# A Strassen step for the second product of a feed-forward block, with attention by thirds of the queries, on one Trainium2 core

## The chip, the core and the metric

The kernel runs on one core of a Trainium2 chip. A core has TensorE (matrix products into PSUM), VectorE, ScalarE and GpSimd (work on columns of 128 partitions), and DMA queues that move data between the device's memory and the on-chip memory. Each engine takes its own instructions in order; they wait for each other through semaphores. The metric is the device time of one execution in microseconds (us), and lower is better.

In the profiles "PE" is TensorE, "PEld" its loading of weights (the stationary operand), "DVE" VectorE, "ACT" ScalarE, "POOL" GpSimd and "SP" the queue that issues the DMAs. "L448" is line 448 of the kernel.

## The reference

Attention with a mask by clusters, then two products with an ELU between. Batch 4, 8 heads, 768 positions, head size 64, 16 clusters, model size 512, inner size 2048, so 3072 tokens in the second part.

```python
def _attn_ref(q, k, v, centroids):
    # q_n, k_n, c_n: rows of q, k, centroids divided by their norms
    q_assign = np.argmax(np.einsum('bhsd,hcd->bhsc', q_n, c_n), axis=-1)
    k_assign = np.argmax(np.einsum('bhsd,hcd->bhsc', k_n, c_n), axis=-1)
    mask = q_assign[:, :, :, None] == k_assign[:, :, None, :]
    scores = scale * np.matmul(q, k.transpose(0, 1, 3, 2))
    scores = np.where(mask, scores, -1000000000.0)
    # softmax over the last axis
    return np.matmul(attn, v)

def _moe_ref(x, w_in, w_out):           # x: (3072, 512)
    h = x @ w_in                        # first product, 512 -> 2048
    g = np.where(h > 0.0, h, np.exp(np.minimum(h, 0.0)) - 1.0)
    return (g @ w_out).astype(np.float32)   # second product, 2048 -> 512
```

The two weight matrices arrive as 64-bit floats, everything else as 32-bit floats. The products run in fp32, but for the mask, which is a product of one-hot rows in bf16.

## The kernel before

The core of it, cut. `b` is the batch, `half` a half of the queries (`HS` = 384), `pr` a pair of heads; `FC` = 16 and `KC` = 4 are the inner and model sizes in blocks of 128, `NT` = 6 the blocks of keys.

The 64-bit weights come in 32 pieces of 128 x 512. Each piece is turned into fp32 by four VectorE, two ScalarE and one GpSimd instruction, with one piece begun while the one before is ended. `ex` has two buffers.

```python
def weight_steps():
    for n in range(len(pieces) + 1) if wide else ():
        if n > 0:
            to = pieces[n - 1][0]
            ex = exps[n - 1]
            nc.scalar.activation(to, to.bitcast(U32), Act.Identity, scale=2.0**-20, bias=one)
            nc.scalar.activation(ex, ex, Act.Relu, scale=8.0, bias=off)
        if n < len(pieces):
            high = words[n][0][:, :, 1]
            e = exps[n] = loads.tile([P, WC], U32, name="ex", tag="ex", bufs=2)
            nc.vector.tensor_scalar(pieces[n][0].bitcast(U32), high, 0xFFFFF, None, op0=Alu.bitwise_and)
            nc.vector.tensor_scalar(e, high, 0x7FF00000, None, op0=Alu.bitwise_and)
        if n > 0:
            w, place, limit = words.pop(n - 1)
            nc.vector.scalar_tensor_tensor(ex, w[:, :, 1], 0x80000000, ex, ...)
            nc.vector.scalar_tensor_tensor(to, w[:, :, 0], 2.0**-52, to, ...)
            nc.gpsimd.tensor_tensor(to, to, ex.bitcast(F32), op=Alu.mult)
            places.append((place, limit))   # the place may take the next piece
            ask()
        yield
```

Attention for block n (batch, half, pair): scores with keys on the partitions, exponentials, the product with v, the row sums (by a product with ones; from pass 6 on VectorE adds the six tiles first), the reciprocal, the scaled result `xT`.

```python
def scores(n):
    for kt in range(NT):
        s = banks()                       # 2 PSUM banks of 512 columns; 3 such pairs
        for e in range(2):                # two heads, on 64 rows of the array each
            nc.tensor.matmul(s[:, e, :HS], lhsT=T[i, 1][rows, ts(kt, P)], rhs=T[i, 0][rows, cols], ...)
        for e in range(2):                # the mask, bf16
            nc.tensor.matmul(s[:, e, :HS], lhsT=hot[b, 1][rows, side(pr, e), ts(kt, P)], rhs=qm[n][rows], ...)
        p = pu[n, kt] = probs.tile([P, 2, HS], F32, name="p", tag="p")
        nc.scalar.activation(p, s[:, :, :HS], Act.Exp, scale=SCALE)

def values(n):
    # ... 12 matmuls of 384 columns into o_bank, 2 (or 12) into d for the row sums
    nc.scalar.copy(x, o_bank[:, :HS])
    nc.scalar.activation(r, d[:, :HS], Act.Copy, accum_out=d_sum[:, n : n + 1])
    nc.vector.reciprocal(r, r)
    nc.gpsimd.tensor_tensor(x, x, r, op=Alu.mult)
```

The feed-forward part of one half of a batch, in four groups of steps:

```python
def hidden(n):                            # 8 of these: 256 inner columns each
    h = banks()
    for ch in range(KC):
        for e in range(2):
            nc.tensor.matmul(h[:, e, :HS], lhsT=w_in[:, ch, ts(2 * n + e, P)], rhs=xT[b * NPR + ch, half], ...)
    t = g[n] = gtp.tile([P, 2, HS], F32, name="gT", tag="gT")
    nc.scalar.activation(t, h[:, :, :HS], Act.Exp)
    nc.gpsimd.tensor_scalar(t, t, 1.0, 0.0, op0=Alu.min, op1=Alu.max)
    finish()                              # the VectorE step of the block before
    lag.append(lambda: nc.vector.scalar_tensor_tensor(t, t, -1.0, h[:, :, :HS], op0=Alu.add, op1=Alu.max))

def outer(t, part):                       # 128 tokens, 4 of 16 inner blocks
    o = f_bank if t == 1 else o_bank
    for f in range(4 * part, 4 * part + 4):
        nc.tensor.matmul(o, lhsT=g[f // 2][:, f % 2, ts(t, P)], rhs=w_out[:, f], ...)   # 512 columns
    if part == 3:
        nc.scalar.copy(o_sb, o)
        nc.sync.dma_start(out[...], o_sb)
```

The loop of passes. A pass runs the values of the block before, the scores of its own block, and the group of feed-forward steps that lies four passes back.

```python
for n in range(len(blocks) + LAG):        # 32 blocks, LAG = 4
    if n <= len(blocks) and n > 0:
        values(n - 1)
    # ... loads of q, k, v ahead
    if n < len(blocks):
        scores(n)
    # ... check(n - 1): a ScalarE sum over r, for a test at the end
    # ... masks(n + 1), sums(n) from n = 6 on, the turning of the next batch's q and k
    main = groups[n - LAG] if n >= LAG else []
    if n < LAG:
        weigh(4)                          # four conversion steps
    for m, step in enumerate(main):
        step()
        # ... a part of the next batch's routing
        if m < 4:
            weigh(2)
```

Of the kernel before, what the change touches and what calls it, by code (L numbers as in the profile page):

```python
# [9 lines left out]
F32 = mybir.dt.float32  # L10
# [8 lines left out]
P = 128  # L19
# [11 lines left out]
def kernel(  # L31
# [24 lines left out]
    with tc.If(good < P):  # L56
        general_path(tc, c, q, k, v, out)
# [3 lines left out]
def main_path(ctx, tc, c, q, k, v, centroids, moe_w_in, moe_w_out, out):  # L61
# [6 lines left out]
    HS = S // 2  # L68
    NPR = H // 2
# [3 lines left out]
    assert D == 64 and NC == 16 and H * NC == P and S % (2 * P) == 0 and DM == H * D and NPR == 4  # L73
# [5 lines left out]
    probs = ctx.enter_context(tc.tile_pool(name="probs", bufs=6))  # L79
    work = ctx.enter_context(tc.tile_pool(name="work", bufs=2))  # L80
    xtp = ctx.enter_context(tc.tile_pool(name="xtp", bufs=6))
    gtp = ctx.enter_context(tc.tile_pool(name="gtp", bufs=FC // 2))
# [11 lines left out]


    pairs = [(b, pr) for b in range(B) for pr in range(NPR)]
    raw = {}
    spare = c["w_out"].rearrange("p f m -> p (f m)")
    used = 0

    def take(n):
        nonlocal used
        used += n
        return spare[:, used - n : used]

    def load(name, i, staged=False):
        b, pr = pairs[i]
        src = {"q": q, "k": k, "v": v}[name]
        if staged:
            t = take(2 * NT * D)  # L110
        else:
            t = loads.tile([P, 2 * NT * D], F32, name=f"{name}_raw", tag=name, bufs=2)
# [27 lines left out]
    for name in "qk":  # L140
        for i in range(NPR):
            load(name, i, staged=i >= 2)
# [49 lines left out]
    r_sum = const.tile([P, 2 * len(pairs)], F32, name="r_sum")  # L192
    d_sum = const.tile([P, 2 * len(pairs)], F32, name="d_sum")
# [70 lines left out]
    for n in range(2):  # L264
        places.append((loads.tile([P, 2 * WC], F32, name="words", tag=f"words{n}"), len(pieces)))
    while used + 2 * WC <= FC * DM:
        limit = into + used // DM - 1
        places.append((take(2 * WC), limit))
# [3 lines left out]
    def weigh(n):  # L272
        for _ in range(n):
            next(rest, None)

# [68 lines left out]
    def masks(n):  # L344
        b, half, pr = blocks[n]
        qm[n] = route.tile([P, HS], BF16, name="qm", tag="qm", bufs=2)
        for e in range(2):
# [4 lines left out]
                hot[b, 0][rows, side(pr, e), half * HS : (half + 1) * HS],  # L352
# [7 lines left out]
    blocks = [(b, half, pr) for b in range(B) for half in range(2) for pr in range(NPR)]  # L360
    pu, osum, xT, rs = {}, {}, {}, {}

    def scores(n):
        b, half, pr = blocks[n]
        i = b * NPR + pr
        cols = slice(half * HS, (half + 1) * HS)
        for kt in range(NT):
            s = banks()
            for e in range(2):
                rows = slice(64 * e, 64 * e + 64)  # L370
                nc.tensor.matmul(  # L371
                    s[:, e, :HS],
                    lhsT=T[i, 1][rows, ts(kt, P)],
                    rhs=T[i, 0][rows, cols],
                    start=True,
                    stop=False,
                )
            for e in range(2):
                rows = slice(64 * e, 64 * e + 64)
                nc.tensor.matmul(  # L380
                    s[:, e, :HS],
                    lhsT=hot[b, 1][rows, side(pr, e), ts(kt, P)],
                    rhs=qm[n][rows],
                    start=False,
                    stop=True,
                )
            p = pu[n, kt] = probs.tile([P, 2, HS], F32, name="p", tag="p")
            nc.scalar.activation(p, s[:, :, :HS], Act.Exp, scale=SCALE)  # L388

    def sums(n):  # L390
        to = osum[n] = work.tile([P, 2, HS], F32, name="psum", tag="psum", bufs=1)
        nc.vector.tensor_tensor(to, pu[n, 0], pu[n, 1], op=Alu.add)
        for kt in range(2, NT):
            nc.vector.tensor_tensor(to, to, pu[n, kt], op=Alu.add)  # L394

    def values(n):

        b, half, pr = blocks[n]
        i = b * NPR + pr
# [3 lines left out]
        def row_sums(p, kt, last):  # L403
            for e in range(2):
                nc.tensor.matmul(  # L405
                    d[64 * e : 64 * e + 64, :HS],
                    lhsT=ones,
                    rhs=p[:, e],
# [4 lines left out]
        for kt in range(NT):  # L413
            for e in range(2):
                nc.tensor.matmul(  # L415
                    o_bank[64 * e : 64 * e + 64, :HS],
                    lhsT=raw["v", n][:, e, kt],
                    rhs=pu[n, kt][:, e],
# [3 lines left out]
            if summed is None:  # L422
                row_sums(pu[n, kt], kt, NT - 1)
        if summed is not None:
            row_sums(summed, 0, 0)
        x = xT[i, half] = xtp.tile([P, HS], F32, name="xT", tag="xT")
        nc.scalar.copy(x, o_bank[:, :HS])  # L427
        r = work.tile([P, HS], F32, name="r", tag="r", bufs=1)
        nc.scalar.activation(r, d[:, :HS], Act.Copy, accum_out=d_sum[:, n : n + 1])  # L429
# [4 lines left out]
    def check(n):  # L434

        seen_r = work.tile([P, HS], BF16, name="seen_r", tag="seen_r", bufs=1)
# [3 lines left out]
    def mlp(b, half):  # L440

        g, lag = {}, []

        def hidden(n):
            h = banks()
            for ch in range(KC):
                for e in range(2):
                    nc.tensor.matmul(  # L448
                        h[:, e, :HS],
                        lhsT=w_in[:, ch, ts(2 * n + e, P)],  # L450
# [15 lines left out]
        def finish():  # L466
            for step in lag:
                step()
# [342 lines left out]
```

## Time and profile before

The time is 1067.61 us (median of three; 1067.3 at the lowest). One of the three took 3830.59 us. The profiled execution has a span of 1067.0 us.

| What | Value | How to read it |
|---|---|---|
| TensorE busy | 1033.4 us, 4211 matmul instructions | busy time is the union of the instructions, which overlap |
| First product, 128x384 | 334.5 us, 1024 instructions | an fp32 matmul is two instructions |
| Second product, 128x512 | 224.6 + 112.8 us, 768 instructions | in two groups, by PSUM bank |
| Scores, fp32 and bf16 | 167.1 + 65.9 us, 768 + 384 instructions | two at a time, on halves of the array's rows |
| Product with v | 136.0 us, 768 instructions | two at a time, on halves of the columns |
| VectorE, ScalarE, GpSimd busy | 418.6, 365.0, 143.5 us | they work in order, so a wait of one step holds all behind it |

The groups of instructions give the mean time of one instruction from its start to its end. For TensorE this is longer than the time from one to the next. The chain of waits follows the run back from its last instruction, at each step to what released it. A table of stretches gives, for a stretch of time, the busy time and the number of instructions of each engine, the granted TensorE clock, the share of DMA and the rate in GB/s.

### The profile page before, as it was taken

Reading aid. Unit: us, or ns where it says so; the run is one execution under the profiler, and the core shown is the slowest. Engines: PE = TensorE matmul, PEld = TensorE weight load, DVE = VectorE, ACT = ScalarE, POOL = GpSimd, SP = SyncE. Lnnn points to the kernel's source line nnn. Section 1 sums busy time; section 2 is a strip of 40 time slices with the busy share of each in tenths; the row PEclk is TensorE's granted clock in tenths of the full one; section 3 lists DMA queues with packets and bytes.
Section 4 is the critical chain, followed back from the end, with each engine's and each line's share of the span. In section 5 each row is a group of like instructions: output and inputs, shape, how many; then the busy total and the mean of one; then the engine's idle time right before and its main releaser. Section 6 shows DMA issues by size and latency. Waiting matters only on the chain.

```text
span 1067.0 us, 10433 instructions
## 1 busy us (share of the span) xinstructions
PE 1033.4 (97%) x4211; PEld 512.3 (48%) x4211; DVE 418.6 (39%) x516; ACT 365.0 (34%) x579; POOL 143.5 (13%) x136
## 2 busy tenths in 40 slices
PE   6979897999999999999999999999999999999997
PEld 4434453445544455445544455444554455444543
DVE  4665856353332343273432134355331233321110
ACT  4876464213332333114333223323331234321100
POOL 0233432001100011001110011000110011100100
PEclk9999898999999999999999999999999999999999
DMA  9374424000202112000202021001000000000000
GB/s 287 97 195 143 117 76 76 25 35 1 45 25 44 47 33 45 25 10 25 45 15 55 35 45 30 25 15 36 15 15 25 20 15 15 16 10 20 1 10 22
DMA packets 99590, 49.01 MB, mean 46 GB/s; under 512 B 83152, under 2 KB 92368, under 8 KB 99536
## 3 DMA queue, kind: packets, MB, share of 16 engines
q1 hardware_dynamic: 99536, 48.28, 17.5%
q8 instruction: 35, 0.57, 0.2%
q14 instruction: 19, 0.16, 0.0%
HBM read 41.98 MB, written 6.29 MB: 45 GB/s over the span
## 4 chain that ended last, share of the span: by engine, by line
PE 89%; DVE 4%; POOL 2%; ACT 2%; issue 1%; DMA 1%; POOLq 0%; ACTq 0%
PE banks L448 29%; PE o_bank L474 21%; PE banks L371 12%; PE f_bank L474 10%; PE o_bank L415 10%; PE banks L380 3%; PE banks L405 2%; PE banks L307 1%; POOL w_out L259 1%; DVE ex L253 1%; POOL w_in L259 1%; DVE ex L250 1%; PE banks L296 1%; ACT p L388 1%; DVE w_out L256 1%
## 5 line engine op out<-in xcount | busy, mean ns | idle before, releaser
L448 PE MATMUL banks<-xT,w_in 128*128 128x384 f32 x1024 | 334.5, 488 | 0.4 <-POOL xT L431 0.4
L448 PEld LDWEIGHTS banks<-xT,w_in 128*128 128x128 f32 x1024 | 193.4, 190 | 139.5 <-issue 7.3
L474 PE MATMUL o_bank<-w_out,gT 128*128 128x512 f32 x512 | 224.6, 596 | 0.0
L430 DVE RECIPROCAL r<-r 128x384 f32<-128x384 f32 x32 | 81.6, 2551 | 295.3 <-ACT r L429 295.3
L371 PE MATMUL banks<-qT,kT 64*128 64x384 f32 x768 | 167.1, 514 | 18.4 <-DVE gT L461 9.9
L388 ACT ACTIVATE p<-banks 128x768 f32<-128x768 f32 x192 | 154.2, 811 | 28.1 <-PE banks L380 28.0
L474 PEld LDWEIGHTS o_bank<-w_out,gT 128*128 128x128 f32 x512 | 96.0, 190 | 122.6 <-issue 122.3
L461 DVE SCALAR_TENSOR_TENSOR gT<-gT,banks 128x768 f32<-128x768 f32 x64 | 61.0, 954 | 215.3 <-POOL gT L458 215.3
L415 PE MATMUL o_bank<-p,v_raw 128*64 128x384 f32 x768 | 136.0, 491 | 0.0
L457 ACT ACTIVATE gT<-banks 128x768 f32<-128x768 f32 x64 | 51.8, 810 | 231.4 <-PE banks L448 231.4
L394 DVE TENSOR_TENSOR psum<-psum,p 128x768 f32<-128x768 f32 x104 | 115.3, 1109 | 11.3 <-DVE psum L394 0.5
L431 POOL TENSOR_TENSOR xT<-xT,r 128x384 f32<-128x384 f32 x32 | 46.5, 1452 | 494.6 <-DVE r L430 494.6
L474 PE MATMUL f_bank<-w_out,gT 128*128 128x512 f32 x256 | 112.8, 593 | 0.0
L371 PEld LDWEIGHTS banks<-qT,kT 64*128 64x128 f32 x768 | 69.9, 196 | 77.1 <-issue 41.2
L458 POOL TENSOR_SCALAR gT<-gT 128x768 f32<-128x768 f32 x64 | 53.9, 843 | 278.7 <-ACT gT L457 278.7
L415 PEld LDWEIGHTS o_bank<-p,v_raw 128*64 128x64 f32 x768 | 52.3, 137 | 77.3 <-issue 76.8
L474 PEld LDWEIGHTS f_bank<-w_out,gT 128*128 128x128 f32 x256 | 48.4, 190 | 61.6 <-issue 61.6
L483 ACT COPY o_sb<-o_bank 128x512 f32<-128x512 f32 x16 | 9.4, 585 | 200.1 <-PE o_bank L474 200.1
L380 PE MATMUL banks<-qm,hot 64*128 64x384 bf16 x384 | 65.9, 332 | 1.0 <-DVE hot L336 1.0
L427 ACT COPY xT<-o_bank 128x384 f32<-128x384 f32 x32 | 15.2, 474 | 130.6 <-PE o_bank L415 130.6
L350 ACT ACTIVATE qm<-hot,minus,big 64x384 bf16<-64x384 bf16 x64 | 44.7, 698 | 4.1 <-DVE hot L336 3.3
L380 PEld LDWEIGHTS <-hot 64*128 64x128 bf16 x384 | 20.3, 97 | 28.7 <-issue 3.3
(88 smaller groups left out, 432.6 us busy)
## 6 DMA issues: line engine op xcount, KB each, us to landing
v_raw<-in_v_dram SPq DMA_DIRECT2D x32, 384.0 KB, 3.2
out_dram<-o_sb SPq DMA_DIRECT2D x24, 256.0 KB, 2.0
w_out<-in_moe_w_in_dram SPq DMA_DIRECT2D x10, 512.0 KB, 5.8
q_raw<-in_q_dram SPq DMA_DIRECT2D x48, 96.0 KB, 3.8
k_raw<-in_k_dram SPq DMA_DIRECT2D x48, 96.0 KB, 3.3
w_out<-in_moe_w_out_dram SPq DMA_DIRECT2D x9, 512.0 KB, 3.5
words<-in_moe_w_out_dram SPq DMA_DIRECT2D x7, 512.0 KB, 3.5
words<-in_moe_w_in_dram SPq DMA_DIRECT2D x6, 512.0 KB, 4.1
```

What stands on the lines that cost most here:

```text
L371: nc.tensor.matmul(s[:, e, :HS], lhsT=T[i, 1][rows, ts(kt, P)], rhs=T[i, 0][rows, cols], start=True, stop=False,)
L380: nc.tensor.matmul(s[:, e, :HS], lhsT=hot[b, 1][rows, side(pr, e), ts(kt, P)], rhs=qm[n][rows], start=False, stop=True,)
L388: nc.scalar.activation(p, s[:, :, :HS], Act.Exp, scale=SCALE)
L394: nc.vector.tensor_tensor(to, to, pu[n, kt], op=Alu.add)
L415: nc.tensor.matmul(o_bank[64 * e : 64 * e + 64, :HS], lhsT=raw["v", n][:, e, kt], rhs=pu[n, kt][:, e], start=(kt == 0), stop=(kt == NT - 1),)
L430: nc.vector.reciprocal(r, r)
L431: nc.gpsimd.tensor_tensor(x, x, r, op=Alu.mult)
L448: nc.tensor.matmul(h[:, e, :HS], lhsT=w_in[:, ch, ts(2 * n + e, P)], rhs=xT[b * NPR + ch, half], start=(ch == 0), stop=(ch == KC - 1),)
L457: nc.scalar.activation(t, h[:, :, :HS], Act.Exp)
L458: nc.gpsimd.tensor_scalar(t, t, 1.0, 0.0, op0=Alu.min, op1=Alu.max)
L461: lambda: nc.vector.scalar_tensor_tensor(t, t, -1.0, h[:, :, :HS], op0=Alu.add, op1=Alu.max)
L474: nc.tensor.matmul(o, lhsT=g[f // 2][:, f % 2, ts(t, P)], rhs=w_out[:, f], start=(f == 0), stop=(f == FC - 1),)
```

## The change

The second product G x W (G: 256 tokens by 2048; W: 2048 by 512) is cut into 2 x 2 blocks and computed with seven block products in place of eight. With G's rows as tokens, G = [[a, b], [c, d]] (blocks of 128 tokens x 1024) and W = [[e, f], [g, h]] (1024 x 256), it needs sums of blocks of W, made once, and sums of blocks of G and of products, made for every 256 tokens. They are put on VectorE, GpSimd and ScalarE. Each block product is 8 matmuls of 256 columns in fp32.

So that 256 tokens come at a time, the queries of a batch are taken in three thirds of 256 in place of two halves of 384. There are 48 blocks of attention in place of 32, each with 256 columns, and scores of two key blocks share a pair of banks, so that an exponential takes 1024 columns. The four hidden blocks of a third have 512 inner columns each. A third's feed-forward part is again four groups: hidden blocks 0 and 1; hidden blocks 2 and 3; block products 1 to 4; block products 5 to 7.

The weights are now all converted before the pass that has the first block products (pass 6): four steps in each of passes 0 to 3, five after each step of passes 4 and 5, and the sums of the weights in pass 6. The 64-bit pieces wait in the space of the weight sums and of the second weight matrix, in 14 places in place of 7. The first batch's q and k wait in the space of g.

The diff, cut to its core:

```diff
+    NQ = 3
+    QS = S // NQ
-    probs = ctx.enter_context(tc.tile_pool(name="probs", bufs=6))
+    probs = ctx.enter_context(tc.tile_pool(name="probs", bufs=NT // 2))
-    gtp = ctx.enter_context(tc.tile_pool(name="gtp", bufs=FC // 2))
+    g = const.tile([P, FC, QS], F32, name="gT")
+    g_sum = const.tile([P, FC // 2, P], F32, name="g_sum")
+    w_sum = const.tile([P, 3, FC // 2, QS], F32, name="w_sum")
 ...
+    def sum_weights(half):
+        of = slice(half * FC // 4, (half + 1) * FC // 4)
+        e_, f_, g_, h_ = (x[:, of] for x in w_parts())
+        t1, t2, t4 = (w_sum[:, n, of] for n in range(3))
+        nc.gpsimd.tensor_tensor(t1, f_, e_, op=Alu.subtract)
+        nc.gpsimd.tensor_tensor(f_, h_, f_, op=Alu.subtract)
+        nc.vector.tensor_tensor(t2, h_, t1, op=Alu.subtract)
+        nc.vector.tensor_tensor(t4, g_, t2, op=Alu.subtract)
 ...
     def scores(n):
-        for kt in range(NT):
+        for u in range(NT // 2):
             s = banks()
+            for m in range(2):
+                kt = 2 * u + m
 ...
+            p = pu[n, u] = probs.tile([P, 2, 2 * QS], F32, name="p", tag="p")
+            nc.scalar.activation(p, s, Act.Exp, scale=SCALE)
 ...
+    def hidden(b, third, n):
+        h = banks()
+        hf = h.rearrange("p a (f s) -> p (a f) s", f=2)
+        for ch in range(KC):
+            for f in range(4):
+                nc.tensor.matmul(hf[:, f], lhsT=w_in[:, ch, ts(4 * n + f, P)], rhs=xT[b, third][:, ch], ...)
+        t = g[:, 4 * n : 4 * n + 4]
+        nc.scalar.activation(t, hf, Act.Exp)
+        nc.gpsimd.tensor_scalar(t, t, 1.0, 0.0, op0=Alu.min, op1=Alu.max)
+        finish()
+        lag.append(lambda: elu(n, t, hf))
+
+    def elu(n, t, hf):
+        nc.vector.scalar_tensor_tensor(t, t, -1.0, hf, op0=Alu.add, op1=Alu.max)
+        if n < 2:      # c becomes a - c
+            nc.vector.tensor_tensor(t[:, :, P:], t[:, :, :P], t[:, :, P:], op=Alu.subtract)
+        else:          # g_sum = d - (a - c)
+            nc.vector.tensor_tensor(g_sum[:, 4 * n - 8 : 4 * n - 4], t[:, :, P:],
+                g[:, 4 * n - 8 : 4 * n - 4, P:], op=Alu.subtract)
+
+    def product(to, left, right, more=False):
+        for f in range(FC // 2):
+            nc.tensor.matmul(to[:, :QS], lhsT=left[:, f], rhs=right[:, f], ...)
+    # outer: seven of these
+    #  1 product(o_bank, a_, e_)              ScalarE copies; VectorE: a_ = g_sum + a_
+    #  2 product(f_bank, c_, f_)              ScalarE copies
+    #  3 product(o_bank, b_, g_, more=True)   ScalarE copies; VectorE: b_ = b_ - g_sum
+    #  4 product(f_bank, d_, t4, more=True)   ScalarE copies
+    #  5 product(f_bank, g_sum, t2)           VectorE adds
+    #  6 product(o_bank, a_, t1)              VectorE and GpSimd add
+    #  7 product(f_bank, b_, h_)              VectorE and GpSimd add, two stores
+
+    def mlp(b, third):
+        steps = [lambda n=n: hidden(b, third, n) for n in range(FC // 4)]
+        yield steps[:2]
+        yield steps[2:] + [finish]
+        yield from outer(b, third)
 ...
         if n < LAG:
             weigh(4)
+        if n == LAG + 2:
+            weigh(100)
+            for half in range(2):
+                sum_weights(half)
 ...
-            if m < 4:
-                weigh(2)
+            if n < LAG + 2:
+                weigh(5)
```

A second path, for inputs that the main path can't take, reloads a part of the second weight matrix, as the sums are made in its place. It isn't taken here.

## The prediction

> **What bounds the kernel now.** I read the granted clock first (one core, 0.990: nothing to correct), then the page's busy times and slices, the chain of waits, and the stretches of time. The page says TensorE is the bound:
>
> ```profile
> PE 1033.4 (97%) x4211; PEld 512.3 (48%) x4211; DVE 418.6 (39%) x516; ACT 365.0 (34%) x579; POOL 143.5 (13%) x136
> PE   6979897999999999999999999999999999999997
> PEclk9999898999999999999999999999999999999999
> PE 89%; DVE 4%; POOL 2%; ACT 2%; issue 1%; DMA 1%; POOLq 0%; ACTq 0%
> ```
>
> The 97% hides two regimes. A table of stretches (length, busy us and count by engine, clock, DMA share, GB/s), cut at the first instruction of the second product (178.45) and at the end of the last big matmul group (1060.20), shows them:
>
> ```profile
> 178.45:1060.20 881.75, 881.39 (x3391) 433.38 (x3390) 305.32 (x322) 258.09 (x414) 87.26 (x83) 1.00 0.10 25
> 0.00:178.45 178.45, 151.93 (x822) 78.92 (x822) 113.09 (x194) 106.35 (x164) 56.23 (x53) 0.94 0.55 148
> ```
>
> After 178.45 TensorE waits for nothing. Before it TensorE is busy for 151.93 of 178.45 us, and part of that at a lower clock (0.94 on the mean). The chain of waits in time order explains it. First a piece of the start, then a piece of the later stretch:
>
> ```profile
> 48.99 1.39 POOL w_in L259
> 52.12 1.39 POOL w_in L259
> 55.24 1.40 POOL w_in L259
> ...
> 144.17 1.39 POOL w_out L259
> ...
> 147.29 1.27 POOL w_out L259
> ...
> 541.59 4.02 PE o_bank L415 x24
> 546.26 0.84 PE banks L371 x4
> 551.30 13.93 PE o_bank L474 x32
> 565.23 6.87 PE f_bank L474 x16
> 572.10 4.02 PE o_bank L415 x24
> ```
>
> In the start the chain runs through the conversion of the 64-bit weights: VectorE, ScalarE, VectorE, GpSimd for each of 32 pieces, one piece per 3.13 us (48.99 to 52.12 to 55.24). Later it is a clock of 572.10 - 541.59 = 30.51 us per pass: attention for one pair of heads and half of the queries, plus a quarter of one half's feed-forward.
>
> **What a matmul of 256 columns costs.** The groups by line and shape give the rates:
>
> ```profile
> L448 PE MATMUL banks<-xT,w_in 128*128 128x384 f32 x1024 | 334.5, 488 | 0.4 <-POOL xT L431 0.4
> L474 PE MATMUL o_bank<-w_out,gT 128*128 128x512 f32 x512 | 224.6, 596 | 0.0
> L448 PEld LDWEIGHTS banks<-xT,w_in 128*128 128x128 f32 x1024 | 193.4, 190 | 139.5 <-issue 7.3
> L371 PEld LDWEIGHTS banks<-qT,kT 64*128 64x128 f32 x768 | 69.9, 196 | 77.1 <-issue 41.2
> ```
>
> Each fp32 matmul is two instructions, and the mean (488, 596) is latency, as they overlap. The throughput comes from the chain: 64 of 384 columns in 20.84 us is 325.6 ns, 48 of 512 columns in 20.80 us (13.93 + 6.87) is 433.3 ns. That is 0.842 ns per column and about 2.5 ns fixed, so 256 columns cost about 217.9 ns. A weight load of 190 ns fits under that, if it starts with the matmul before it.
>
> **What the Trainium skill says.** "TensorE: Matmul & The Clock Gate", section "Back-to-back issue gap", has a fixed part of about 2.5 ns per matmul when warm; the two rates above agree. Its section "Step-by-step: what each phase is for" says that the next weights load while a matmul runs; the trace agrees, since 190 ns loads cost nothing beside 325.6 ns matmuls, though no run so far shows 256 columns. Its section "HAM oscillation — how this bites in real kernels" says that a gap of over about 3.4 us puts the clock back to half; the trace agrees, with a clock of 0.94 in the start and 1.00 after. "SBUF — State Buffer", section "Who interferes with whom", says that a VectorE instruction with two SBUF inputs contends with GpSimd's reads; the trace agrees: GpSimd's multiply of 128x384 takes 1.0 us in the start and 1452 ns on the mean of all 32.
>
> **The change, part by part, after the start.** *Second product:* before 8 half-batches x 41.6 us = 333 us. After: 12 thirds x 7 block products x 8 x 2 instructions = 1344 of 217.9 ns = 292.9 us. Saved: 40 us. *First product:* before 1024 x 325.6 = 333.4 us, after 1536 x 217.9 = 334.7 us: nothing. *Attention:* before 30.55 - 20.84 = 9.71 us per pass, of which 26 pairs of fp32 (row or column halves of the array run together) at 0.322 and 6 bf16 pairs at 0.163 are 9.36, so 0.35 us is changeover. After: 26 x 0.216 + 6 x 0.109 + 0.35 = 6.61 us per pass, 48 passes for 32: 317 us for 311, a loss of 6.5 us. One doubt: a bf16 pair of 256 columns lasts 109 ns and must hide an fp32 weight load, whose streaming part I put at (190 - 137) / 64 x 128 = 106 ns from the loads of 128 and of 64 columns (137 ns). It just fits; I add 0 to 8 us to the range for it.
>
> *Sums on the other engines:* per third VectorE gets 4 adds of 512, 2 of 1024 and 3 of 256 columns from PSUM: by the row of 895 ns for 768 columns about 2.5 + 2.4 + 1.1 = 6 us per third, 72 in all. It goes from 39% to under 50%. ScalarE gets 4 copies, GpSimd 2 adds. Each is read two or more block products (3.5 us each) later, except the last: after the end of TensorE there is now a VectorE and a GpSimd add in place of one copy (0.585 us), about +1 us. Between hidden blocks one bank pair is held into the next pass, so scores turn over two pairs instead of three; an Exp of 1024 columns (about 1.03 us from 811 ns for 768) against 1.08 us of matmuls just keeps up. So after the start TensorE stays the bound.
>
> **The start is what I think decides.** It is set by the 32 conversions, which are not reduced. In the same passes TensorE now has a third less attention and a third less first product to do under them, and that work comes later. Then the first block sums of the weights wait for the last piece. I follow ScalarE, which does everything in program order:
> - Pass 0 ends at about 38 us as before (38.11).
> - Passes 1 to 3: before 16.5 us each (38.11, 54.62): four conversion steps 8.4, the end of their chain 3.6, reciprocal 2.55, check 0.7, masks 1.4. With 256 columns: 8.4 + 3.6 + 1.7 + 0.6 + 1.1 = 15.3. Pass 4 starts at 84.
> - Pass 4: hidden block 0 done at 95; then ten steps, 10 x 3.13 us, and two Exp with their clamp and maximum (1 to 1.5 us each, from the 7.0 us that two steps and one block take before): pass 5 starts at about 125.
> - Pass 5: scores and hidden block 2 take it to 138.5 (before, 16.8 us passed from the start of the pass to its first hidden Exp; here I get 13), then seven steps and a block, 7 x 3.13 + 1.5, less the overlap at the end: about 162 for the last weight.
> - Pass 6: reciprocal and x to about 166. Then GpSimd makes four sums of 1024 columns: its 512 columns take 1274 to 1383 ns, so 2.6 to 3.2 us each, 11.5 us: 177.5. The second block product needs the last of them; it ends at about 179.5 with the half clock after the gap. Two products of 3.48 us should have ended then, so the effective start of the second product is 172.5.
>
> From there: 11 hidden thirds x 27.89 + 12 outer thirds x 24.40 + 41 passes of attention x 6.61 + 3.3 + three changes of batch x 2.86 = 882 us. The same sum for the kernel before, from 178.45, is 30 x 20.80 + 25 x 9.75 + 4.9 + 8.6 = 881.3, against 881.75 in its table of stretches, so the method holds. Sum: 172.5 + 882 + 7.5 (before 6.8 after the last matmul) = 1062; I round to 1060, as I took the slower of two readings at several steps.
>
> So the 40 us saved are nearly spent: 6.5 on shorter attention matmuls, and about 30 because less of TensorE's work lies under the conversions.
>
> **Rivals.** *(1) The start shrinks with the work:* the conversions run faster as less attention is beside them, and the second product starts at 150. Then 1038. For it: passes are shorter. Against: the 3.13 us step is its own loop, with nothing of attention in it. *(2) Weight loads show at 256 columns:* 20 ns on each of some 4000 would give 1140. For it: 190 is near 217. Against: loads of 190 start beside the matmul and only their streaming part blocks. *(3) VectorE or the two-slot banks become the bound* in the hidden passes: 1 us per pass, 1110. Against: VectorE has 305 us of 882 in the stretch. *(4) DMA:* 14 pieces are asked for at once ahead of the next v tile. In the first slice 287 GB/s move, so 11 MB land by about 39 us and v is first needed at 53: hidden.
>
> **Range and chances.** The start is uncertain by some 10 us either way, the weight loads by +8, the rest by 4. So 1060, from 1042 to 1078. Faster by over 2% means under 1046.3, which needs the second product to start by 157: 0.17. Slower by over 2% means over 1089, which needs rival 2 or 3: 0.07.
>
> **What would show it.** Stretches of the new kernel: TensorE fully busy from about 180 on, and 880 us long; the first block product at about 165 and a gap of several us before the end of the second, released by GpSimd. Matmuls of 256 columns 216 to 218 ns apart; if they are 230 or more, rival 2. A last weight before 145 would make me wrong on the start (rival 1). TensorE idle in the hidden passes after 200 us would be rival 3.

## The result, and the profile after

The changed kernel takes 1081.84 us (median of four, 1081.20 to 1083.77) against 1067.83 us for the kernel before beside it: a ratio of 1.0136, interval 1.0116 to 1.0156. It is slower, by less than 2%. The prediction was 1060 with a range up to 1078, so it was 22 us too low and its range missed: it foresaw a kernel some 8 us faster, and the change made it 14 us slower.

The page of the changed kernel, the lines that answer to those of before (busy time by engine; TensorE's busy tenths and granted clock in 40 slices; shares of the chain of waits):

```profile
PE 1012.6 (94%) x6323; PEld 782.4 (73%) x6323; DVE 500.1 (46%) x624; ACT 381.9 (35%) x651; POOL 163.9 (15%) x164
PE   6778477999999999999999999999999999999996
PEclk9989688999999999999999999999999999999999
PE 82%; DVE 9%; POOL 4%; issue 2%; ACT 2%; DMA 0%; POOLq 0%; ACTq 0%
```

TensorE is busy for 20.8 us less (1033.4 before), and the span is 11.2 us longer: it is idle for 65.6 us in place of 33.6. The low digits stand in the first seven slices alone, and the granted clock is down there too. Two stretches (length, busy us and count of PE, PEld, DVE, ACT and POOL, clock, DMA share, GB/s), the first up to where the second product would begin if nothing held it up, the second from within the third block product to the end of the last one:

```profile
0.00:174.60 174.60, 121.27 (x845) 83.66 (x845) 109.97 (x193) 92.91 (x147) 64.14 (x53) 0.86 0.47 142
182.73:1070.15 887.42, 885.77 (x5463) 694.77 (x5462) 381.60 (x419) 288.67 (x503) 95.76 (x109) 1.00 0.14 34
```

174.60 is reckoned back from the end of the fourth block product, 188.58, as four of them take 14.0 us later on (one of 3.65 and three of 3.45). In the first stretch TensorE is idle for 53.3 of 174.6 us; before it was 26.5 of 178.45. So 26.8 of the 32 us of new idle time lie in the start. After it TensorE is full again, at full clock. The chain of waits in time order (start, length, what) shows who leads in the start:

```profile
46.22 1.39 POOL w_in L264
...
49.34 1.39 POOL w_in L264
...
52.46 1.40 POOL w_in L264
...
160.21 1.27 POOL w_out L264
...
163.77 1.58 POOL xT L460
165.35 3.29 POOL w_sum L296
168.71 2.67 POOL w_out L297
171.38 3.29 POOL w_sum L296
174.74 3.21 POOL w_out L297
178.00 2.53 PE f_bank L511 x8
180.53 4.60 PE o_bank L511 x16
185.13 3.45 PE f_bank L511 x16
188.58 2.74 PE o_bank L442 x24
...
212.40 14.01 PE banks L481 x64
226.41 2.74 PE o_bank L442 x24
...
233.34 14.01 PE banks L481 x64
247.35 2.74 PE o_bank L442 x24
```

The conversion goes on at 3.12 us a step as before (46.22, 49.34, 52.46), its last weight comes at 161.5, and then GpSimd's four sums of weights (12.5 us from 165.35 to 177.95) hold the second block product. Later the chain is TensorE alone: one pass with hidden blocks from 226.41 to 247.35 is 20.94 us. Of it 14.01 us are 64 instructions of 256 columns, 218.9 ns each, and 16 in 3.45 us are 215.6 ns. The groups (PE matmul, PEld weight load; busy us, mean ns) show that the loads of 190 ns stay beside them:

```profile
L481 PE MATMUL banks<-xT,w_in 128*128 128x256 f32 x1536 | 338.4, 381 | 1.3 <-DVE gT L498 1.3
L481 PEld LDWEIGHTS banks<-xT,w_in 128*128 128x128 f32 x1536 | 290.5, 190 | 47.8 <-ACT p L415 3.2
```

So the story of the prediction is in the trace: the start is bound by the conversion, the rest by TensorE. What remains is whether the conversion really swallows the gain, and why the sum came out too small.

### The profile page after: what moved, and what is told of

It is laid out like the page before. It is cut to its first block, busy times and chain, and to the rows that moved or that the text cites. A ratio compares the mean times of both kernels' runs of the same rounds, so it can differ in the third digit from the quotient of the medians.

```text
span 1078.2 us, 14856 instructions
## 1 busy us (share of the span) xinstructions
PE 1012.6 (94%) x6323; PEld 782.4 (73%) x6323; DVE 500.1 (46%) x624; ACT 381.9 (35%) x651; POOL 163.9 (15%) x164
## 4 chain that ended last, share of the span: by engine, by line
PE 82%; DVE 9%; POOL 4%; issue 2%; ACT 2%; DMA 0%; POOLq 0%; ACTq 0%
PE banks L481 30%; PE f_bank L511 15%; PE o_bank L511 12%; PE banks L398 11%; PE o_bank L442 10%; PE banks L407 3%; PE banks L431 2%; POOL w_out L264 2%; POOL w_in L264 1%; DVE ex L258 1%; DVE oh L351 1%; PE banks L332 1%; DVE hot L361 1%; DVE ex L255 1%; DVE w_in L261 1%
## 5 line engine op out<-in xcount | busy, mean ns | idle before, releaser
L481 PE MATMUL banks<-xT,w_in 128*128 128x256 f32 x1536 | 338.4, 381 | 1.3 <-DVE gT L498 1.3
L481 PEld LDWEIGHTS banks<-xT,w_in 128*128 128x128 f32 x1536 | 290.5, 190 | 47.8 <-ACT p L415 3.2
L398 PE MATMUL banks<-qT,kT 64*128 64x256 f32 x1152 | 176.7, 404 | 38.1 <-ACT r L458 27.4
L415 ACT ACTIVATE p<-banks 128x1024 f32<-128x1024 f32 x144 | 147.0, 1025 | 46.8 <-PE banks L407 42.4
L459 DVE RECIPROCAL r<-r 128x256 f32<-128x256 f32 x48 | 84.0, 1750 | 161.8 <-ACT r L458 161.7
L442 PE MATMUL o_bank<-p,v_raw 128*64 128x256 f32 x1152 | 141.4, 386 | 0.0
L498 DVE SCALAR_TENSOR_TENSOR gT<-gT,banks 128x1024 f32<-128x1024 f32 x48 | 58.4, 1216 | 163.0 <-POOL gT L492 163.0
L492 POOL TENSOR_SCALAR gT<-gT 128x1024 f32<-128x1024 f32 x48 | 50.9, 1060 | 317.1 <-ACT gT L491 317.1
L511 PE MATMUL f_bank<-w_out,gT 128*128 128x256 f32 x384 | 89.8, 387 | 7.9 <-POOL w_out L297 7.9
L511 PE MATMUL o_bank<-w_out,gT 128*128 128x256 f32 x384 | 89.1, 386 | 0.0
L407 PE MATMUL banks<-qm,hot 64*128 64x256 bf16 x576 | 83.8, 277 | 2.8 <-DVE hot L361 2.8
```

The lines of the kernel that those rows point to most:

```text
L398: nc.tensor.matmul(s[:, e, ts(m, QS)], lhsT=T[i, 1][rows, ts(kt, P)], rhs=T[i, 0][rows, cols], start=True, stop=False,)
L407: nc.tensor.matmul(s[:, e, ts(m, QS)], lhsT=hot[b, 1][rows, side(pr, e), ts(kt, P)], rhs=qm[n][rows], start=False, stop=True,)
L415: nc.scalar.activation(p, s, Act.Exp, scale=SCALE)
L442: nc.tensor.matmul(o_bank[64 * e : 64 * e + 64, :QS], lhsT=raw["v", n][:, e, kt], rhs=p[:, e, ts(m, QS)], start=(kt == 0), stop=(kt == NT ...
L481: nc.tensor.matmul(hf[:, f], lhsT=w_in[:, ch, ts(4 * n + f, P)], rhs=xT[b, third][:, ch], start=(ch == 0 and f % 2 == 0), stop=(ch == KC - 1),
L498: nc.vector.scalar_tensor_tensor(t, t, -1.0, hf, op0=Alu.add, op1=Alu.max)
```

## The experiments

Unless a run says otherwise it is an edit of the changed kernel. "Theory A" is that the conversion of the 64-bit weights sets the end of the start, so that work taken off TensorE turns into idle time there. The rivals differ by run.

### Without the conversion, after and before

One VectorE instruction for each piece stands for the seven of a conversion step (the weights then have wrong values). In both kernels:

```diff
-            ...  # 2 ScalarE, 4 VectorE and 1 GpSimd instruction for each piece
+        for n in range(len(pieces)):
+            w, place, limit = words.pop(n)
+            nc.vector.tensor_scalar(pieces[n][0].bitcast(U32), w[:, :, 1], 0xBFFFFFFF, None, op0=Alu.bitwise_and)
+            places.append((place, limit))
+            ask()
+            yield
```

Of the changed kernel:

> The changed kernel with the conversion of the weights left out (one VectorE instruction of 0.4 us per piece takes its place, and the weights are wrong). Theory A, the start set by the conversions hides the gain: the first block product then starts near 110 us instead of 162.6, the sums of the weights still hold the second one up by about 10 us, and the time is 1026 us, or 0.96 of the kernel before. Theory B, the block products themselves save little: it stays within 15 us of the changed kernel's 1082 less what the kernel before gains by the same edit.

Of the kernel before:

> The kernel before with the same left out. Theory A: its start is then set by TensorE, whose work up to 178.45 us is about 151 us, so it gains some 27 us and takes 1041 us: 15 us more than the changed kernel without conversion, so the order of the two turns round. Theory B: the changed kernel stays the slower of the two, by about 14 us as with conversion.

Measured: 1026.08 us after and 1040.01 us before, ratios to the kernel before of 0.9608 (0.9592 to 0.9624) and 0.9742 (0.9725 to 0.9758), both as theory A has it. Without the conversion the changed kernel is 14 us the faster one; with it, 14 us the slower one. The busy times of the two, after and then before, in spans of 1023.3 and 1038.1 us:

```profile
PE 999.8 (98%) x6323; PEld 778.5 (76%) x6323; DVE 445.6 (44%) x528; ACT 340.6 (33%) x587; POOL 117.3 (11%) x132
```

```profile
PE 1023.3 (99%) x4211; PEld 508.1 (49%) x4211; DVE 361.6 (35%) x420; ACT 324.8 (31%) x515; POOL 100.2 (10%) x104
```

The change does take work off TensorE, 23.5 us by these pages. Not all of it reaches the time, as GpSimd's sums of the weights still hold the second block product in the changed kernel (until 122.71 us on its chain). That the conversion decides whether the change is seen as a gain or a loss is shown.

### Thirds without the seven products

The changed kernel with the old second product, two groups of 128 tokens for each third, and no sums of blocks:

```diff
-        product(o_bank, a_, e_) ...  # seven block products and their sums
+        def tokens(t):
+            o = f_bank if t == 1 else o_bank
+            for f in range(FC):
+                nc.tensor.matmul(o, lhsT=g[:, f, ts(t, P)], rhs=w_out[:, f], ...)
+            nc.scalar.copy(o_sb, o)
-            for half in range(2):
-                sum_weights(half)
```

> Attention by thirds and the new schedule of the conversions, but the second product as before, 512 columns at a time, with no sums of blocks. Theory A: 12 thirds x 3.4 us come back (+40), and the wait for the sums of the weights in pass 6 goes (-12): 1110 us. Theory B: under 1095.

Measured: 1120.36 us, 1.0491 (1.0474 to 1.0509). So the preparation alone costs 52.6 us, and the seven products give 38.5 us of it back, near the 40 that were counted for them. Its second product starts at 161.92 us by its trace, so the sums of weights cost the changed kernel about 12.7 us of start. Of the 10 us over the expectation some 7 have another cause (an estimate, 12 thirds x 0.59 us): in its trace TensorE waits for ScalarE's copy of 0.59 us in a third (260.03 on the chain), as the values of the next pass write the bank that the copy reads. The seven products end in the other bank and don't meet this wait.

### The sums of weights in another order

h - f first, its halves shared by VectorE and GpSimd, as the second block product needs it:

```diff
+        for half, eng in ((0, nc.vector), (1, nc.gpsimd)):
+            e_, f_, g_, h_, t1, t2, t4 = parts[half]
+            eng.tensor_tensor(f_, h_, f_, op=Alu.subtract)
+        for e_, f_, g_, h_, t1, t2, t4 in parts:
+            nc.vector.tensor_tensor(t2, f_, e_, op=Alu.add)
+            nc.vector.tensor_tensor(t4, g_, t2, op=Alu.subtract)
+        for e_, f_, g_, h_, t1, t2, t4 in parts:
+            nc.gpsimd.tensor_tensor(t1, h_, t2, op=Alu.subtract)
```

> The changed kernel with the same sums of the weights in another order: h - f first, one half on VectorE and one on GpSimd, then the others from it. Theory A with the wait on GpSimd in pass 6 as a part of it: the second block product ends at 171.8 us instead of 180.5 and the time falls by 9 to 11 us, to 1072. If the wait is covered by another one, under 3 us.

Measured: 1076.59 us, 1.0088 (1.0072 to 1.0105), so 5.3 us less, half of what was expected. The chain of this run:

```profile
162.90 1.66 DVE r L466
...
165.75 1.57 DVE psum L427
...
167.34 2.71 DVE psum L428
170.05 1.15 DVE w_out L301
...
171.24 5.21 PE f_bank L518 x16
```

The wait has moved: VectorE's half of h - f (L301) now stands behind the reciprocal and the sums of rows of its own queue, and one of these sums (L428) takes 2.71 us where its median over the run is 0.69, with GpSimd at work beside it.

### Four places for ex, after and before

In the kernel before it is one number; in the changed kernel, which has no room, two of the places lie in the tile of the row sums.

```diff
-                e = exps[n] = loads.tile([P, WC], U32, name="ex", tag="ex", bufs=2)
+                e = exps[n] = loads.tile([P, WC], U32, name="ex", tag="ex", bufs=4)
```

> The changed kernel with four buffers for the exponents of the weights in place of two (two of them in the space of the row sums, which are idle until pass 6). Theory A: the step of the conversion is a loop through one exponent buffer, 3.13 us; with four it is bound by VectorE's four instructions, 2.2 to 2.5 us, so 32 steps save some 20 us and the time is 1062 us. Rival C, the step is set by an engine and not by the buffers: under 4 us.

> The kernel before with four buffers for the exponents. Theory A: its start is bound by the same loop, up to the point where TensorE's own work of about 151 us sets it, so it gains about 19 us: 1049 us, and stays ahead of the changed kernel by some 13 us. Rival C: no gain.

Measured: 1079.28 us after (1.0111, 1.0089 to 1.0134) and 1064.60 before (0.9964, 0.9950 to 0.9978), so 2.6 and 3.3 us less, and not 20 (the first is not clear of noise, as its interval overlaps with that of the changed kernel). That a step waits for a free ex was wrong as the reason for its length: the wait went, and the step went only from 3.12 to 2.95 us. The instruction behind the wait shows why (VectorE's, for the exponent bits; count, and least, median and greatest ns). In the changed kernel, and then with four places:

```profile
L255 DVE TENSOR_SCALAR ex<-w_sum x19: 412/427/958, 28.1 to 156.2; 128x512 uint32<-128x512 uint32 x19
L255 DVE TENSOR_SCALAR ex<-w_out x13: 415/427/953, 50.8 to 122.2; 128x512 uint32<-128x512 uint32 x13
```

```profile
L260 DVE TENSOR_SCALAR p_sum<-w_sum x10: 414/1492/1521, 34.9 to 154.6; 128x512 uint32<-128x512 uint32 x10
L260 DVE TENSOR_SCALAR ex<-w_sum x9: 419/1487/1508, 28.9 to 146.0; 128x512 uint32<-128x512 uint32 x9
```

It starts a microsecond earlier and takes a microsecond longer. One of them in the run with four places, with GpSimd's multiply beside it (start, length, what):

```profile
46.63 1.38 POOL L269 TENSOR_TENSOR w_in<-w_in,p_sum 128x512 f32<-128x512 f32 x1 [3.55 <-DVE w_in L266]
46.80 1.50 DVE L260 TENSOR_SCALAR ex<-w_sum 128x512 uint32<-128x512 uint32 x1
```

The multiply begins first and ends at 48.01 us, and VectorE's instruction ends 0.3 us behind it. The Trainium skill, "SBUF — State Buffer", section "Who interferes with whom", says that VectorE in its two-port modes and GpSimd shut each other out for a whole instruction, and that whoever issues first has the ports. The trace agrees in the order and the size of the hold-up (427 to about 1490 ns), though no run shows in which mode this instruction works. The run with that multiply on VectorE, below, tests whether GpSimd is what holds it up.

### The held banks, and the routing

Each is an edit of a line or two. The pass of hidden blocks 0 and 1 ends the VectorE step of its second block itself, so that no bank pair is held into the next pass:

```diff
-        yield steps[:2]
+        yield steps[:2] + [finish]
```

> The changed kernel with the last VectorE step of the first hidden group done in its own pass, so that no pair of banks is held into the next. The pass after it should take 20.6 us instead of 20.94: 12 x 0.33 = 4 us less, 1078. If the extra 0.3 us has another cause, no change.

and at a change of batch the assignments and the masks are asked for one block product earlier:

```diff
             upto = len(beside) * (m + 1) // len(main)
+            if len(main) == 3 and beside:
+                upto = (3, 6, 6)[m]
```

> The changed kernel with the routing of the next batch moved one block product earlier in the three passes that have it. There TensorE waits for VectorE's assignment of the keys, 21.96 us from the fifth block product to the next hidden block against 17.2 elsewhere, of which 2.9 are its own matmuls: 3 x 1.9 us less, 1076.

Measured: 1080.01 (1.0112, 1.0094 to 1.0131) and 1081.22 (1.0126, 1.0109 to 1.0143), so 1.8 and 0.6 us less. The passes did what was expected. Of the first, the chain:

```profile
228.75 2.74 PE o_bank L442 x24
...
235.38 14.01 PE banks L481 x64
249.39 2.74 PE o_bank L442 x24
```

That is 20.64 us from pass to pass where it was 20.94, ten times over. In the second the pass after a change of batch goes from 21.53 to 20.64 us, three times. What they save in the passes (3.0 and 2.7 us) shows only in part in the time, because in both profiled runs the values of pass 7 begin about 2 us later (190.85 and 190.6 for 188.51), though the code of the start is the same in the second. The start is not the same in every execution: of the four of the changed kernel, two with a mean clock of 0.973 took 1081.2 and 1081.5 us and two with 0.969 took 1082.2 and 1083.8, while all four of the second run had 0.969. So single differences of this size are read from the passes and not from the time.

### The routing left out

For the size of the changes of batch as a whole, batches 1 to 3 take the one-hot rows of batch 0 and have no routing of their own (their masks are others then):

```diff
-                beside.append(lambda b=b, j=j: [similar(b + 1, j, half) for half in range(2)])
-                beside.append(lambda b=b, j=j: [assign(b + 1, j, half) for half in range(2)])
+                hot[b + 1, j] = hot[b, j]
 ...
```

> The changed kernel without the routing of batches 1 to 3: their products with the centroids and VectorE's assignments are left out and the one-hot rows of batch 0 stand in for them (so the masks of these batches are others). If the seams are worth what the passes of the changed kernel show: the two passes at a seam go from 21.07 and 21.53 us to about 17.2 and 20.65, three times 4.75 us, so 1066 to 1069 us. Rival (the passes after a seam get slower in turn, as TensorE's lead over VectorE is spent there): 1074 or more. What then stays over the predicted steady sum is the held banks and the rate of the passes.

Measured: 1067.27 us, 0.9995 (0.9985 to 1.0005), so 14.6 us less. The chain of the two passes at the change of batch:

```profile
268.69 2.74 PE o_bank L443 x24
...
285.88 2.74 PE o_bank L443 x24
...
306.52 2.74 PE o_bank L443 x24
```

17.19 and 20.64 us, for 21.07 and 21.53 in the changed kernel: 4.77 us each time, 14.3 in all. The rival, that later passes get slower in turn, falls; each third is 79.41 us, as elsewhere.

### What is gained with the start mended

Five kernels ask whether the seven products pay once the start is less of a bound. The first is the changed kernel with four of the edits above: four places for ex, the sums reordered (h - f also before pass 6), the held banks freed, the routing earlier. The second also moves ScalarE's sum over the reciprocal behind the conversion steps in passes 1 to 5; the third is the kernel before with four places for ex and this move. The fourth and fifth are the second and third with the multiply of a conversion step on VectorE.

```diff
+        if n == LAG + 2:
+            weigh(100)
+            sum_weights(0)         # h - f
-        if 0 < n <= len(blocks):
+        if LAG + 2 <= n <= len(blocks):
             check(n - 1)
 ...
+        if 0 < n < LAG + 2:        # at the end of the pass
+            check(n - 1)
 ...
-                nc.gpsimd.tensor_tensor(to, to, ex.bitcast(F32), op=Alu.mult)
+                nc.vector.tensor_tensor(to, to, ex.bitcast(F32), op=Alu.mult)
```

The four edits:

> The changed kernel with four edits at once: four places for ex (two of them in the space of the sums of rows), the block h - f formed first and before pass 6 begins, VectorE and GpSimd sharing the sums of the weights, the fourth hidden step of VectorE ended in the third pass of a third's four (no bank pair held), and the routing of the next batch drawn earlier. Theory A (each edit removes its own wait and they add up, as measured singly: 5.3, 2.5, 1.8 and 0.6 us, up to 3.3 and 2.7 for the last two where the start does not vary): 1066 to 1071 us. Theory B (the conversion chain sets the start and swallows all but the steady part): 1076.

(The text above has the held banks in another pass than the edit: it is the one shown before, in the pass of blocks 0 and 1.)

Measured: 1066.44 us, 0.9987 (0.9978 to 0.9996), within the range of theory A. That is 15.4 us less and more than the 10.3 us of the single runs added up; the 6 us or so of the passes (held banks and routing) are now seen in full, and the second product starts at 164.93, straight behind the scores.

With the late sum, after and before:

> As e9, and in passes 1 to 5 ScalarE's sum over the reciprocal of the pass before is asked for at the end of the pass and not ahead of the masks and the conversion steps, so that ScalarE no longer waits there for the 1.75 us reciprocal and the values ahead of it. Theory A (in passes 1 to 3 the conversion waits some 3 to 5 us each for that chain): about 12 us less than e9, the last weight before 152 us, 1052 to 1060. Theory B (the four steps of a pass end at the same time whatever stands before them, since the chain through the next scores brings them back): within 3 us of e9.

> The kernel before with four places for ex and the same move of ScalarE's sum to the end of passes 1 to 5. If theory A of e10 holds: about 10 us less than with four places alone (1064.6), so 1052 to 1057. Theory B: 1063 to 1066. The comparison with e10 says whether the seven products give a faster kernel than the eight once both starts are mended: by the steady parts alone (882 before; 895.5 less about 10 after) the changed one should be some 5 to 10 us slower or equal.

Measured: 1061.31 us after (0.9928, 0.9909 to 0.9947), 5.1 us less than the run above, so between the two theories; and 1063.01 before (0.9948, 0.9928 to 0.9967), 1.6 us less than with four places alone (not clear of noise), which is theory B. The kernel before has another wait. Its chain:

```profile
152.84 3.51 DMA words<-in_moe_w_out_dram
...
159.55 5.05 DMA words<-in_moe_w_out_dram
...
167.51 1.65 PE banks L371 x4
```

It has seven places for the pieces, and its late steps wait for pieces of the second weight matrix to land. The changed kernel with its 14 places has no such piece on its chain there. A transfer of this kind stands on the chain of the kernel before itself too (4.27 us at 164.93). No run changes the number of places alone, so that this is the reason is not shown.

With the multiply on VectorE, after:

> As e10, and the multiply that ends a conversion step goes from GpSimd to VectorE, so that no GpSimd instruction holds VectorE's one-input instruction up (1.41 us in place of 0.43 us). VectorE then has five instructions a step, about 0.43 + 0.43 + 0.63 + 0.63 + 0.6 = 2.7 us. Theory A (the held-up instruction sets the step of 2.95 us): steps of 2.6 to 2.8 us, some 3 to 8 us less than e10. Theory B (two engines are better than one; VectorE becomes the bound with its other work in those passes): a step of 3 us or more, the same time as e10 or slower.

Measured: 1056.75 us, 0.9897 (0.9880 to 0.9913), 4.6 us less than the run with the late sum, as theory A has it. The instruction that was held up:

```profile
L260 DVE TENSOR_SCALAR p_sum<-w_sum x10: 418/420/946, 35.5 to 131.8; 128x512 uint32<-128x512 uint32 x10
L260 DVE TENSOR_SCALAR ex<-w_sum x9: 417/422/953, 28.8 to 125.0; 128x512 uint32<-128x512 uint32 x9
```

Back at 0.42 us from 1.49, and a step is 2.60 us (two of these instructions begin at 35.53 and 38.13), although VectorE now does five of its seven instructions. So GpSimd's multiply was what held it up. TensorE's longest waits in this start are now 12.36 us (up to 116.32) and 8.75 us (up to 127.57), and from there to the second product it waits for nothing. In the stretch that ends there VectorE is busy for 37.05 of 37.57 us (columns as above), so it is now the engine that the start waits for:

```profile
90.00:127.57 37.57, 11.80 (x79) 7.02 (x77) 37.05 (x68) 18.85 (x33) 1.14 (x1) 0.62 0.38 103
```

The same before:

> The kernel before with the edits of e11 and the multiply of a conversion step on VectorE, as in e12. e11 ended its last step at 180.0 us and its trace has TensorE waiting from 161.6 to 167.5 us for the pass before. Theory A (the conversion steps still set its start): about 2.6 us a step in place of 2.95, 8 to 12 us less, 1051 to 1055 us, faster than e12 (1056.75), so eight products would be as good as seven. Theory B (the start is set by when the 64-bit pieces of the second weight matrix land, as it has 7 places for them and not 14; the chain of e11 has a transfer of such a piece of 5 us in it at 159.55 us): 1060 to 1063 us, and e12 stays faster.

Measured: 1055.18 us, 0.9881 (0.9864 to 0.9897). Theory A held: 7.8 us less than with the late sum alone, and the fastest of all that leave nothing out, though the intervals of the last two overlap. A transfer is still on its chain, so the pieces' landing is a part of its start and did not bound it alone:

```profile
154.59 4.00 DMA words<-in_moe_w_out_dram
```

The starts of the two, cut at their first block of the second product, after and then before (columns as above):

```profile
0.00:154.43 154.43, 111.41 (x822) 77.06 (x822) 119.63 (x221) 87.80 (x141) 12.06 (x19) 0.87 0.52 161
```

```profile
0.00:165.63 165.63, 146.09 (x822) 74.96 (x822) 127.37 (x223) 104.21 (x164) 13.87 (x22) 0.98 0.58 159
```

TensorE is idle in the start for 43.0 us with the seven products and for 19.5 us with the eight. In the whole spans of 1054.7 and 1053.9 us it is busy for 1001.0 and 1027.7 us. So with both starts mended the change saves 26.7 us of TensorE and adds 27.5 us of idle time, 23.5 of it in the start and 4 behind the last product: the gain is all lost again, most of it in the same place.

## Why the prediction was wrong

**The direction of the mechanism was right.** The prediction said that the 40 us saved would be nearly spent on less work under the conversions. Idle time in the start rose by 26.8 us for the "about 30" it named, and the two runs without the conversion turn the order of the kernels round. The rival of a shrinking start (1) fell: the step stayed 3.12 us. So did the weight loads (2): 256 columns came every 215.6 to 218.9 ns, for 217.9 reckoned, and a bf16 pair took 0.11 us. (That only a part of a load blocks, as (2) has it, no run shows.) The banks (3) were not a bound but cost 3.0 us. The loads ahead of v (4) don't show on the chain.

**The start was right in its steps.** Pass 4 was put at 84 and began at 82.6; pass 5 at 125 and began at 123.3; the first block of pass 5 was put at 138.5 and ended at 137.0; the last weight at 162 and came at 161.5; the last sum of weights at 177.5 and came at 177.95. The second block product was to end at 179.5 and ended at 180.53, and the third, after the gap, took 4.60 us in place of 3.45. So the effective start is 174.6 for 172.5, 2.1 us later. In one place this is luck: the terms of pass 4 (95, then 31.3, then 2 to 3) add up to over 128 and not to 125.

**The step that failed is the sum after the start**: "882 us", which is 895.5 in the trace, from 174.6 to 1070.15. Its terms:

| Term | Put at | Measured | Difference over the stretch |
|---|---|---|---|
| Three changes of batch | 3 x 2.86 = 8.6 | 14.3 (left out, by itself) | +5.7 |
| Bank pair held between the hidden groups | 0 ("just keeps up") | 0.30 a third, freed by itself | +3.0 |
| Four passes of a third, the rest | 27.89 + 24.40 + 26.44 = 78.73 | 79.11 | +4 |

That makes 12.7 of the 13.5 us. The first two were tested alone. For the change of batch the prediction took 2.86 us from the kernel before. There it is the two products with the centroids alone, and the pass that has them is 33.76 us long:

```profile
199.25 4.02 PE o_bank L415 x24
...
216.03 1.43 PE banks L307 x16
...
224.52 1.43 PE banks L307 x16
...
233.01 4.02 PE o_bank L415 x24
```

That is 3.25 us over the 30.51 of such a pass without them, as the block products around them are slower. The check of the method against 881.75 hides this: it has 9.75 us for a pass of attention, where the working and the trace have 9.71, and the two differences cancel. In the changed kernel a change of batch costs 4.77 us. The pass with the products takes 3.88 us more, with 2.06 us for the first of them:

```profile
278.27 2.06 PE banks L332 x16
```

VectorE's assignment of the keys is not done in that pass of 21.07 us, as it was in the 33.76 us before, and the next pass waits for its masks (0.89 us). Both went when the routing was left out; why the first product takes 2.06 us is open. The third term is 1 ns or so for each instruction of 256 columns (218.9 for 217.9 in the hidden blocks) and 0.03 us for each pass of attention; it was read from the trace alone. A sum of some 5400 instructions is no better than its rate: half a per cent is 4 us, and the method's fit to the kernel before (881.3 for 881.75) came from rates that were fitted to that kernel.

**The end** was put at 7.5 us, from the 6.8 us between the last product and the end of the span. The time goes on behind the span: from the last product to the end of the time it is 8.7 us in the profiled execution of the kernel before (1060.20 to 1068.89) and 11.7 us in the changed kernel (1070.15 to the median of 1081.84), so +4.2. Of the 3 us more the trace shows some 2: VectorE's test at the end had been made ahead of the last product, and now stands in VectorE's order behind the last addition. Its last instruction begins 2.05 us after the last product (1072.20), for 0.13 us before (1060.33). No run tests this, and the rest is open. With the start and the sum that makes 2.1 + 13.5 + 4.2 = 19.8 us, from the reckoned 1062 to the measured 1081.8. Taking 2 us off for "the slower of two readings" was a step without a measurement behind it, and in the wrong direction.

**The range** gave "the rest" 4 us either way, and that is where nearly all of the error was: every neglected term in the sum had the same sign.

## What to carry to other kernels

Before a saving on the bound engine is counted, ask in which stretch the work lies that is taken away and what it covered there: here 21 to 27 us less on TensorE came back as 24 to 27 us of waiting in the start. A rate that was fitted to one tiling holds for the other to about half a per cent, and terms that were hidden under long passes (routing, held banks) come out when the passes get shorter, so give each a cost above zero. And mend the start before the bulk: three edits of the conversion and its neighbours gave the kernel before some 13 us (1068.51 to 1055.18), more than the seven products gave in any pair of versions with the conversion in them (at best 1.7 us, 1061.31 for 1063.01, not clear of noise).

## What was not expected of the hardware

- A VectorE instruction with one input, 0.427 us alone, took 1.49 us beside GpSimd's multiply, so two engines at once needed 2.95 us a step where VectorE with the multiply of its own (0.69 us for GpSimd's 1.38) needed 2.60.
- TensorE's granted clock averaged 0.86 over the start of the changed kernel, for 0.94 before. The Trainium skill, "TensorE: Matmul & The Clock Gate", section "HAM oscillation — how this bites in real kernels", says that gaps of over about 3.4 us bring half the clock. The trace agrees: after its first matmul TensorE has seven waits longer than that in this start (3.69 to 10.70 us) and the kernel before has two (4.18 and 5.68 us), and the clock is 1.00 in the stretch without gaps. After the wait of 5.09 us in the second block product, half of that product took 3.78 us, where half of a later one takes 1.73:

```profile
171.43 3.78 PE L511 MATMUL f_bank<-w_out,gT 128*128 128x256 f32 x8 [5.09 <-POOL w_out L297]
```

- In two traces with the same code in the start the steady part begins 2.1 us apart (188.51 and 190.6 us).
